# The inverse transform of a spectral layer by pairs of tiles, with two of its products as 64x64 products

## The chip, the core and the metric

The kernel runs on one core of one Trainium2 chip. The metric is the device time of one execution in microseconds (us); lower is better. The engines are named as in the profile: PE (TensorE matmul), PEld (its weight load), DVE (VectorE), ACT (ScalarE), POOL (GpSimd), SP (SyncE, which issues the DMAs).

## The reference

`x` is 2048 x 576 (S x D), in float32. The layer computes

```
def _A_ref(x, w_r, w_i):                      # spectral mixing
    X = rfft2(x)                              # over S and D: 2048 x 289 complex
    X = X * (w_r + 1j * w_i)
    return irfft2(X, s=(S, D))
def _B_ref(x, w1, w2):                        # MLP, Dff = 4608
    return maximum(x @ w1, 0) @ w2
h  = x + _A_ref(layernorm(x), w_r, w_i)
h2 = h + _B_ref(layernorm(h), w1, w2)         # the output
```

## The kernel before

The 2048 rows are held as 16 tiles (t = 0 to 15) of 128 partitions; a partition is 64 * j + h, with j = 0 or 1 the half of the tile. The FFTs are products with small matrices of cosines and sines (float32). All of the program stands in one order written by hand: each engine works through its own queue in the order of the source, and an instruction that waits holds up all that is behind it on its engine.

The program has five stages:

- the forward row transform, to 46 us;
- the middle stage (`mid_d`, `mid_b`, `mid_i`, lines 332 to 375), which transforms along D and the rest of S, multiplies by W and goes back along S; its products write column halves of 64. `mid_i` writes its result to `U` with one ACT copy for each of 16 steps (L375);
- the inverse stage (115.8 to 222.5 us, loop L641 to L673), which the change rewrites;
- plain MLP steps to 286 us;
- MLP slots with Winograd-like products (`slot`, L577) to 1046 us, and the last stores.

In the inverse stage each tile goes through these steps:

- `inv_d(t)` (L400): two PSUM halves (r = 0, 1), each the sum of a product with the 64 leftover frequencies (`lpv`, 290 columns; for r = 0 only rows 0 to 63 of it are not zero, for r = 1 only rows 64 to 127) and two with the 128 main frequencies (`dev`, 145 columns each). ACT copies the first half of each (helper L151), DVE makes difference and sum (L415, L416) and half of `y` (L419), POOL the other half of `y` (L418).
- `inv_a(t)` (L422): the row stage, `cai` (128 x 128, two 64 x 64 blocks on the diagonal, zero elsewhere) times `y`, in two products of 288 columns; DVE adds the result to `xs`, the reloaded x (L428).
- `stat2(t)` (L432): statistics of the layer norm, on DVE (L208, L209), and for every second tile the rsqrt and shift on POOL (L211 to L214).
- `norm2` (L436): the normalised tile, by ACT (L222).
- `project(t)` (L442): five transposes on PE (L446, L447); ACT copies the high part (5 x 128 columns) and a full copy (4 x 128), POOL makes the low part (L454), DVE a rest of 64 rows (L455).
- `mm1(i, a)` (L460) and `mm2(i, tt)` (L485): layer 1 and layer 2 of the MLP for weight group g and chunk c of four tiles. A product is made of three (high x high, high x low, low x high): the first product of layer 1 reads a high part that ACT wrote, the second a low part that POOL wrote.

The loop runs over t = 0 to 21: `inv_d(t)`, the start of `norm2` for a pair, `stat2(t - 3)`, `inv_a(t - 1)`, from t = 10 to 21 one unit of the MLP (two calls of `mm1` to a chunk, in two tile-iterations, then `mm2`), `project(t - 6)`, and the weight splits at t = 2, 4, 18 and 19. So layer 1 of a chunk starts a tile-iteration after the projection of the chunk's last tile. Matmuls and element-wise steps of one form have one line each in helpers: L148 is every matmul but transposes, L151 every plain ACT copy.

Buffers: PSUM has four tiles "d" of two banks, taken in turn (`ps()`), so a tile is free once its last reader four takes ago is done. "e" is a ring of ten SBUF buffers. `U` has the tag "X", which the second weight group's buffer takes over at t = 15.

Of the kernel before, what the change touches and what calls it, by code (L numbers as in the profile page):

```python
# [16 lines left out]
S, D, DFF = 2048, 576, 4608  # L17
NK = D // 2 + 1
NT = 16
# [4 lines left out]
CH = 4  # L24
# [103 lines left out]
def kernel(ctx: ExitStack, tc: tile.TileContext, x, w_r, w_i, w1, w2, cc2, c1, fb, ib, c3, out):  # L128
    nc = tc.nc
# [7 lines left out]
    n = [0]  # L137

    def ps():
        n[0] += 1  # L140
        return psum.tile([128, 1024], F32, tag="d", name=f"d_{n[0]}", bufs=4)

    def ebuf(shape, dt=F32):
        e = sb([128, EW], "e", EB, dt)[:, :int(np.prod(shape[1:]))]
        return e.rearrange("p (a b) -> p a b", a=shape[1]) if len(shape) == 3 else e

    def mm(o, l, r, start, stop):
        nc.tensor.matmul(o, l, r, start=start, stop=stop)  # L148

    def act(o, i, **kw):  # L150
        nc.scalar.activation(o, i, AF.Copy, **kw)  # L151
# [16 lines left out]
    caf, cai = ccs[:, :384], ccs[:, 384:]  # L168
# [194 lines left out]
    def mid_i(p):  # L363
        Y = Ys.pop(p)
        pu = ps()
        for e in range(2):
            ibe = IB[p // 4][:, p % 4, e, :]
            for h in range(2):
                for g in range(2):
                    mm(pu[64 * g:64 * g + 64, 512 * e + 128 * h:512 * e + 128 * h + 128],  # L370
                       dims(Y, NK * e + 128 * g + h, [2, 64]), ibe, True, True)
            for g in range(2):
                mm(pu[64 * g:64 * g + 64, 512 * e + 256:512 * e + 320],
                   dims(Y, NK * e + 225, [1, 64]), ibe[:, 64 * g:64 * g + 64], True, True)
        act(dims(U, 2 * p, [32, 2], [64, 160], [1, 2]), dims(pu, 0, [512, 2], [2, 160], [1, 2]))  # L375

    for i in range(NP + 2):
        if i < NP:
# [19 lines left out]
    Es = {}  # L398

    def inv_d(t):  # L400
        pd = ps()
        ut = [dims(U, 64 * (32 * b + 2 * t), [1, 128]) for b in range(5)]
# [5 lines left out]
        ez = ebuf([128, 578 + D])  # L408
# [6 lines left out]
        nc.vector.tensor_sub(dims(ez, 288, R2, [-1, 144]), ea[:, :, :144], pb_[:, :, :144])  # L415
        nc.vector.tensor_add(ea, ea, pb_)  # L416
        y = ez[:, 578:]
        nc.gpsimd.tensor_sub(dims(ez, 578 + 575, [-1, 287]), e0[:, 1:288], e1[:, 1:288])  # L418
        nc.vector.tensor_add(y[:, 0:289], e0, e1)  # L419
        Es[t] = y  # L420

    def inv_a(t):  # L422
        y = Es.pop(t)
        pa = ps().rearrange("p (h n) -> p h n", h=2)[:, :, :288]
        for h in range(2):
            mm(pa[:, h], cai, y[:, 288 * h:288 * h + 288], True, True)
        xt = xs[:, t, :].rearrange("p (h n) -> p h n", h=2)
        nc.vector.tensor_add(xt, xt, pa)  # L428
# [12 lines left out]

    def project(t):  # L442
        y = Zs.pop(t)
        pz = ps()
        for b in range(4):
            nc.tensor.transpose(pz[:, 128 * b:128 * b + 128], y[:, 128 * b:128 * b + 128], ident)  # L446
        nc.tensor.transpose(pz[:, 512:640], y[:, 448:576], ident)  # L447
# [4 lines left out]
        zt = ebuf([128, 512])  # L452
        act(zt, pz[:, :512])
        nc.gpsimd.tensor_sub(dst[:, 5:9, q], zt.rearrange("p (a s) -> p a s", s=128), dst[:, 0:4, q])  # L454
        nc.vector.tensor_sub(dst[0:64, 4, q], pzv[64:128, 4], dst[64:128, 4, q])  # L455
# [4 lines left out]
    def mm1(i, a, part=None):  # L460
        g, c = steps[i]
        w1h, w1l = wts[g, 0]
        if a == 0 and not part:
            pend[i] = None if i >= WINO else ps()
        p = hid_p(i, a) if i >= WINO else pend[i][:, 512 * a:512 * a + 512]
        f = slice(128 * a, 128 * a + 128)
        ops = []
        for kt in range(4):
            ops += [(w1h, kt, kt), (w1h, kt, 5 + kt), (w1l, kt, kt)]
        ops += [(w1h, 4, 4), (w1l, 4, 4)]  # L470
        for n_, (w, kt, xk) in enumerate(ops):
            if part is None or n_ // 7 == part:
                mm(p, w[:, kt, f], xc[c][:, xk, :], n_ == 0, n_ == len(ops) - 1)
        if i >= WINO:
            return
        if a == GF - 1:
            p = pend.pop(i).rearrange("p (a s) -> p a s", a=GF)
            hh, hl = sb([128, GF, 512], "D", 4, F32R), sb([128, GF, 512], "D", 4, F32R)
            nc.scalar.activation(hh, p, AF.Relu)
            nc.vector.scalar_tensor_tensor(hl, p, 0.0, hh, op0=ALU.max, op1=ALU.subtract)  # L480
            hid[i] = (hh, hl)
# [88 lines left out]

    def store(c, hs, hd):
        if steps[-1][0] == NG - 1:
            for j in range(2):
                t, d = CH * c + 2 * hs, slice(288 * hd, 288 * hd + 288)
                nc.sync.dma_start(ov[j, :, t:t + 2, d], xs[64 * j:64 * j + 64, t:t + 2, d])

    def slot(i):  # L577
        g, c = steps[i]
# [61 lines left out]
    gen = None  # L640
    for t in range(NT + 6):  # L641
        if t < NT:
            inv_d(t)
        if t % 2 == 1 and 5 <= t <= NT + 3:
            gen = norm2(t - 5, 2)
            next(gen)
        if 0 <= t - 3 < NT:
            stat2(t - 3)
        if 0 <= t - 1 < NT:
            inv_a(t - 1)  # L650
        if t == 15:
# [3 lines left out]
        if t == 17:  # L655
            project(t - 6)
        if 10 <= t < 22:
            i, u = divmod(t - 10, 4)
            if u < 2:
                mm1(i, u)  # L660
            else:
                if i == 2:
                    mm1(3, u - 2)
                mm2(i, 2 * u - 4)
                mm2(i, 2 * u - 3)
        if 6 <= t and t != 17:
            project(t - 6)
        if t in (2, 4):
            split_weights(0, t // 2 - 1)
        if t in (18, 19):  # L670
            split_weights(1, t - 18)
        if gen:
            next(gen, None)  # L673
# [49 lines left out]
```

## Time and profile before

| | |
|---|---|
| median of three runs | 1055.14 us (1054.94 to 1055.36) |
| profiled execution | 1053.18 us |
| its span | 1051.1 us |
| PE busy | 1033.6 us, 98% |
| DVE, ACT, POOL busy | 71%, 37%, 31% |
| chain that ended last, PE's share | 94% |

The span runs from the first to the last instruction of the profiled execution; its own time is 2.1 us longer. In rows of a timeline the first number is the start in us, the second the length; products that follow each other on PE overlap a little, so the distance of two starts is what a product takes of PE's time. A bracket names the idle time before the row and what ended it.

### The profile page before, as it was taken

To read this page: it belongs to the slowest core of one execution; us is meant where nothing else is said; L and a number is where in the kernel's file an instruction comes from. 1 tells how busy PE (TensorE), PEld (TensorE's weight loads), DVE (VectorE), ACT (ScalarE), POOL (GpSimd) and SP (SyncE) were. 2 spreads that over 40 slices of the span, in tenths; PEclk is the share of its full clock that TensorE was granted. 3 is DMA by queue.
4 is the path that set the end of the run, shared out by engine and by line. 5 is a ranking of instruction groups with operands and counts; after the bars stand their busy time and mean duration, and the time that the engine had idled before them with its cause. 6 is when DMAs were issued, how large, how long until landed. Compare 5 with 4: busy or idle time off the path is not lost.

```text
span 1051.1 us, 17190 instructions
## 1 busy us (share of the span) xinstructions
PE 1033.6 (98%) x6560; PEld 924.6 (88%) x6560; DVE 751.3 (71%) x1411; ACT 389.9 (37%) x846; POOL 325.7 (31%) x436
## 2 busy tenths in 40 slices
PE   8999999999999999999999999999999999999997
PEld 7878778799999999999999999999999999999996
DVE  7587686544377777778777777778777777777775
ACT  4533243521134333333333333334343333434332
POOL 4300164311132324333333423333333323243321
PEclk9999999999999999999999999999999999999999
DMA  8931700011000110000000011000000001000025
GB/s 241 249 89 49 181 2 26 23 48 49 1 26 23 28 47 23 26 23 26 23 26 23 26 30 42 26 23 26 24 26 23 26 24 46 29 23 2 1 63 118
DMA packets 31073, 48.05 MB, mean 46 GB/s; under 512 B 2960, under 2 KB 22672, under 8 KB 30992
## 3 DMA queue, kind: packets, MB, share of 16 engines
q1 hardware_dynamic: 30992, 46.96, 16.3%
q8 instruction: 52, 0.85, 0.3%
q14 instruction: 29, 0.24, 0.1%
HBM read 42.23 MB, written 4.72 MB: 45 GB/s over the span
## 4 chain that ended last, share of the span: by engine, by line
PE 94%; DVE 2%; DMA 2%; ACT 1%; POOL 0%; issue 0%; SPq 0%; ACTq 0%; DVEq 0%; POOLq 0%
PE d L148 59%; PE d L562 34%; DMA A<-in_A_x_dram 2%; PE d L446 1%; DVE st L208 0%; DVE A L428 0%; ACT e L222 0%; DMA X<-in_A_x_dram 0%; SPq L159 0%; DVE e L307 0%; POOL r L212 0%; DVE e L252 0%; PE d L447 0%; DVE e L253 0%; DVE e L416 0%
## 5 line engine op out<-in xcount | busy, mean ns | idle before, releaser
L569 DVE TENSOR_TENSOR A<-A,d 128x576 f32<-128x576 f32 x448 | 334.5, 747 | 50.5 <-PE d L562 50.2
L562 PE MATMUL d<-X,D 128*128 128x288 f32 x2304 | 346.2, 294 | 1.4 <-DVE A L569 0.9
L562 PEld LDWEIGHTS d<-X,D 128*128 128x128 f32 x2304 | 329.0, 188 | 17.2 <-DVE A L569 1.1
L148 PE MATMUL d<-B,e 128*128 128x512 f32 x952 | 238.3, 391 | 0.4 <-DVE A L428 0.4
L148 PEld LDWEIGHTS d<-B,e 128*128 128x128 f32 x952 | 172.0, 188 | 28.7 <-ACT e L151 0.8
L537 DVE SCALAR_TENSOR_TENSOR D<-d,D 128x256 fp32r<-128x256 f32 x192 | 81.5, 424 | 122.0 <-ACT D L536 122.0
L536 ACT ACTIVATE D<-d 128x256 fp32r<-128x256 f32 x192 | 73.4, 382 | 239.6 <-PE d L148 239.6
L551 POOL TENSOR_TENSOR e<-e 128x256 f32<-128x256 f32 x64 | 47.3, 739 | 355.3 <-ACT e L550 355.3
L148 PE MATMUL d<-C,e 128*128 128x512 f32 x476 | 119.1, 390 | 0.0
L148 PE MATMUL d<-X,e 128*128 128x512 f32 x476 | 118.8, 390 | 0.0
L151 ACT ACTIVATE X<-e 128x288 fp32r<-128x288 f32 (+2 forms) x177 | 70.2, 434 | 105.6 <-PE d L562 105.6
L307 DVE TENSOR_TENSOR D<-e,D 128x512 fp32r<-128x512 f32 (+1 forms) x128 | 92.7, 724 | 19.9 <-ACT D L151 19.9
L547 POOL TENSOR_TENSOR e<-e 128x256 f32<-128x256 f32 x64 | 47.6, 744 | 173.6 <-ACT e L546 173.6
L148 PEld LDWEIGHTS d<-X,e 128*128 128x128 f32 x476 | 85.9, 188 | 13.7
L148 PEld LDWEIGHTS d<-C,e 128*128 128x128 f32 x476 | 85.8, 188 | 13.7
L151 ACT ACTIVATE D<-e 128x512 fp32r<-128x512 f32 (+1 forms) x128 | 66.7, 521 | 75.5 <-POOL e L552 71.9
L307 DVE TENSOR_TENSOR X<-e,X 128x288 fp32r<-128x288 f32 (+2 forms) x177 | 83.1, 492 | 0.9 <-ACT X L151 0.9
L562 PEld LDWEIGHTS d<-X 128*128 128x128 f32 x384 | 58.0, 188 | 5.1
L562 PE MATMUL d<-X 128*128 128x288 f32 x384 | 61.4, 295 | 0.0
L148 PE MATMUL d<-e,D 128*128 128x288 f32 x384 | 53.8, 297 | 0.3 <-DVE D L480 0.3
L148 PEld LDWEIGHTS d<-e,D 128*128 128x128 f32 x384 | 52.2, 188 | 1.4 <-DVE D L480 0.6
L552 POOL TENSOR_TENSOR e<-e,e 128x256 f32<-128x256 f32 x64 | 50.4, 788 | 5.0
(79 smaller groups left out, 986.9 us busy)
## 6 DMA issues: line engine op xcount, KB each, us to landing
e<-in_B_w_dram SPq DMA_DIRECT2D x18, 576.0 KB, 3.8
e<-in_B_w_dram SPq DMA_DIRECT2D x18, 512.0 KB, 3.6
A<-in_A_x_dram SPq DMA_DIRECT2D x16, 288.0 KB, 8.4
out_dram<-A SPq DMA_DIRECT2D x32, 144.0 KB, 2.5
X<-in_A_x_dram SPq DMA_DIRECT2D x12, 288.0 KB, 7.1
e<-in_B_w_dram SPq DMA_DIRECT2D x36, 64.0 KB, 3.4
B<-in_A_w_r_dram SPq DMA_DIRECT2D x15, 144.5 KB, 8.1
B<-in_A_w_i_dram SPq DMA_DIRECT2D x15, 144.5 KB, 7.0
```

The lines of the kernel that those rows point to most:

```text
L148: nc.tensor.matmul(o, l, r, start=start, stop=stop)
L151: nc.scalar.activation(o, i, AF.Copy, **kw)
L307: nc.vector.tensor_sub(l, v, h)
L446: nc.tensor.transpose(pz[:, 128 * b:128 * b + 128], y[:, 128 * b:128 * b + 128], ident)
L536: nc.scalar.activation(h, p, AF.Relu)
L537: nc.vector.scalar_tensor_tensor(l, p, 0.0, h, op0=ALU.max, op1=ALU.subtract)
L547: nc.gpsimd.tensor_sub(fs["S3"], fs["p0"][:, 0], fs["p0"][:, 1])
L551: nc.gpsimd.tensor_add(fs["S1"], fs["p0"][:, 1], fs["p1"][:, 1])
L552: nc.gpsimd.tensor_sub(fs["S2"], fs["S1"], fs["p0"][:, 0])
L562: nc.tensor.matmul(P[:, tt], l[:, q], r, start=first and n_ == 0, stop=n_ == 2, skip_group_check=not first)
L569: nc.vector.tensor_add(xt, xt, P)
```

## The change

The inverse stage goes by pairs of tiles, and two kinds of products become 64 x 64.

- **Leftover frequencies** (`left` in the new `inv_h`): the two products of a tile with `lpv` that multiplied zero rows too become four of 64 x 64: row half r of `U`'s leftover block, column half m. Each has 290 columns.
- **Row stage** (`row`): `cai`'s two blocks are used one by one, for both tiles of the pair, as four 64 x 64 products of 288 columns: row half j, column half j for an even tile, and exchanged for an odd one. `row(0)` and `row(1)` each issue four that lie in the four quarters. The rows of odd tiles hold their halves exchanged from there to the store.
- **Where things lie**: `U` is laid out by tile (640 columns each), so `mid_i` writes it with four ACT copies of 160 columns in place of one of 640 (L375, new L377). `y` is written back into the tile's block of `U`. Two tiles share a buffer "e" for the inverse, and two for the projection.
- **x reload**: 16 DMAs as before, each for 64 partitions and two tiles, now tiles t and t + 2.
- **Store**: each DMA for two tiles becomes two for one tile each, 64 in place of 32.
- **Order**: the loop runs over u = 0 to 9, with `inv_h(u)` (leftover product of the new even tile, first half of the row stage of the old pair, leftover product of the new odd tile, second half of the row stage, residual adds), `norm2` of pair u - 2, `inv_d` of both new tiles, `stat2` of both tiles of pair u - 1, weight splits at u = 1, 2 and 8, `project` of both tiles of pair u - 2, and for u = 3 to 8 two units of the MLP.

The core of the diff:

```diff
-        act(dims(U, 2 * p, [32, 2], [64, 160], [1, 2]), dims(pu, 0, [512, 2], [2, 160], [1, 2]))
+        for e in range(2):
+            for j in range(2):
+                act(dims(U, 64 * j + 32 * e + 2 * p, [128, 5], [640, 16], [1, 2]),
+                    dims(pu, 512 * e + 2 * j, [64, 5], [4, 16], [1, 2]))
...
-    for k in range(8):
-        load_x(xs, 2 * k, 2)
+    def rows(t, j):
+        k = 64 * (j ^ t % 2)
+        return slice(k, k + 64)
+    for t in range(0, NT, 4):
+        for o in range(2):
+            for j in range(2):
+                nc.sync.dma_start(xs[rows(o, j), t + o:t + o + 3:2, :], xv[j, :, t + o:t + o + 3:2, :])
...
+    def inv_h(u):
+        new = [2 * u, 2 * u + 1] if 2 * u < NT else []
+        old = [2 * u - 2, 2 * u - 1] if u else []
+        pa = {}
+        def left(t):
+            pds[t] = ps()
+            for r in range(2):
+                for m in range(2):
+                    mm(pds[t][64 * m:64 * m + 64, 512 * r:512 * r + 290],
+                       U[64 * r:64 * r + 64, 640 * t + 512 + 64 * m:640 * t + 576 + 64 * m], lpv[64 * r:64 * r + 64, r], True, False)
+        def row(k):
+            for j in range(2):
+                for t in old:
+                    h = j ^ k
+                    mm(pa[t][rows(t, j), 512 * h:512 * h + 288], cai[64 * j:64 * j + 64, 64 * j:64 * j + 64],
+                       inv_y(t)[64 * j:64 * j + 64, 288 * h:288 * h + 288], True, True)
+        for t in new[:1]:
+            left(t)
+        for t in old:
+            pa[t] = ps()
+        row(0)
+        for t in new[1:]:
+            left(t)
+        row(1)
+        for t in old:
+            xt = xs[:, t, :].rearrange("p (h n) -> p h n", h=2)
+            nc.vector.tensor_add(xt, xt, pa[t].rearrange("p (h n) -> p h n", h=2)[:, :, :288])
...
-            mm(o, ut[4], lpv[:, r], True, False)
...
-        y = ez[:, 578:]
-        nc.gpsimd.tensor_sub(dims(ez, 578 + 575, [-1, 287]), e0[:, 1:288], e1[:, 1:288])
+        y = inv_y(t)
+        nc.gpsimd.tensor_sub(dims(y, 575, [-1, 287]), e0[:, 1:288], e1[:, 1:288])
...
-                nc.sync.dma_start(ov[j, :, t:t + 2, d], xs[64 * j:64 * j + 64, t:t + 2, d])
+                for o in range(2):
+                    nc.sync.dma_start(ov[j, :, t + o, d], xs[rows(o, j), t + o, d])
...
+    for u in range(NT // 2 + 2):
+        inv_h(u) if u <= NT // 2 else None
+        if 2 <= u:
+            for _ in norm2(2 * u - 4, 2):
+                pass
+        if 2 * u < NT:
+            inv_d(2 * u)
+            inv_d(2 * u + 1)
+        if 1 <= u <= NT // 2:
+            stat2(2 * u - 2)
+            stat2(2 * u - 1)
+        if u in (1, 2):
+            split_weights(0, u - 1)
...
+        if u == 8:
+            split_weights(1, 0)
+            split_weights(1, 1)
+        if u >= 2:
+            project(2 * u - 4)
+            project(2 * u - 3)
+        if 3 <= u < 9:
+            unit(2 * u - 6)
+            unit(2 * u - 5)
```

How the order of instructions changes is seen at two places. First POOL's queue around the projection of a chunk's last tiles, before: L454 makes a low part of layer 1's input, L418 half of `y` of an inverse tile, L211 to L214 the rsqrt and shift of a pair.

```order
L454 TENSOR_TENSOR B_1285<-e_1658,B_1285 128x4x128
L418 TENSOR_TENSOR e_1670<-e_1670 128x287
L211 TENSOR_SCALAR r_1625<-mv_1624 128x2
L212 TENSOR_TENSOR r_1625<-r_1625,half_141 128x2
L214 TENSOR_SCALAR r_1625<-mv_1624,r_1625 128x1 x2
L454 TENSOR_TENSOR B_1285<-e_1722,B_1285 128x4x128
L418 TENSOR_TENSOR e_1734<-e_1734 128x287
L454 TENSOR_TENSOR B_1285<-e_1786,B_1285 128x4x128
L418 TENSOR_TENSOR e_1798<-e_1798 128x287
```

The same place after the change (L464 is the half of `y`, L493 the low part):

```order
L464 TENSOR_TENSOR X_551<-e_1778 128x287 x2
L211 TENSOR_SCALAR r_1795<-mv_1794 128x2
L212 TENSOR_TENSOR r_1795<-r_1795,half_141 128x2
L214 TENSOR_SCALAR r_1795<-mv_1794,r_1795 128x1 x2
L493 TENSOR_TENSOR B_1333<-e_1813,B_1333 128x4x128 x2
L464 TENSOR_TENSOR X_551<-e_1889 128x287 x2
```

Before, low parts and halves of `y` alternate tile by tile, and every fourth step the rsqrt stands between them; after, both halves of `y` of a pair come first, then the rsqrt of the pair ahead of it, then both low parts of the pair that is projected.

Second, PE's queue ahead of a layer 1, with the engines that each instruction waits for, before: L446 and L447 are a tile's transposes, the products with X an inverse tile, those with cc the row stage, those with B the start of layer 1.

```order
L446 MATMUL d_1779<-ident_62,e_1622 128x128 [waits DVE_49,Activation_49]
L446 MATMUL d_1779<-ident_62,e_1622 128x128 x3
L447 MATMUL d_1779<-ident_62,e_1622 128x128
L148 MATMUL d_1791<-e_549,X_551 128x290 [waits DVE_49]
L148 MATMUL d_1791<-e_549,X_551 128x145 x2
L148 MATMUL d_1791<-e_549,X_551 128x290
L148 MATMUL d_1791<-e_549,X_551 128x145 x2
L148 MATMUL d_1811<-e_1734,cc_73 128x288 [waits DVE_49]
L148 MATMUL d_1811<-e_1734,cc_73 128x288 [waits Pool_49]
L148 MATMUL d_1815<-B_1285,e_1334 128x512 [waits DVE_49,Activation_49]
L148 MATMUL d_1815<-B_1285,e_1334 128x512 [waits Pool_49]
L148 MATMUL d_1815<-B_1285,e_1335 128x512
```

And after (the main products of two inverse tiles, L483 and L484 for the transposes of two tiles, then layer 1):

```order
L148 MATMUL d_1749<-e_549,X_551 128x145 x4
L148 MATMUL d_1760<-e_549,X_551 128x145 x4
L483 MATMUL d_1806<-ident_62,e_1771 128x128 [waits DVE_49,Activation_49]
L483 MATMUL d_1806<-ident_62,e_1771 128x128 x3
L484 MATMUL d_1806<-ident_62,e_1771 128x128
L483 MATMUL d_1817<-ident_62,e_1771 128x128 [waits DVE_49,Activation_49]
L483 MATMUL d_1817<-ident_62,e_1771 128x128 x3
L484 MATMUL d_1817<-ident_62,e_1771 128x128
L148 MATMUL d_1827<-B_1333,e_1418 128x512 [waits DVE_49,Activation_49]
L148 MATMUL d_1827<-B_1333,e_1418 128x512 [waits Pool_49]
L148 MATMUL d_1827<-B_1333,e_1419 128x512
```

Before, an inverse tile and the row stage of another stand between the last transposes and layer 1; after, layer 1 follows directly on the transposes of the chunk's last two tiles.

More of the change, by code (lines that the diff above doesn't have):

```diff
@@ L397, with inv_y @@
     xc = [xc01[:, 0], xc01[:, 1], xc2]
-    Es = {}
+    pds, Ez = {}, {}
+    def inv_y(t):
+        return U[:, 640 * t:640 * t + D]
+    def inv_h(u):
[25 more added lines that the diff above has]
+            nc.vector.tensor_add(xt, xt, pa[t].rearrange("p (h n) -> p h n", h=2)[:, :, :288])
     def inv_d(t):
-        pd = ps()
-        ut = [dims(U, 64 * (32 * b + 2 * t), [1, 128]) for b in range(5)]
+        pd = pds.pop(t)
+        ut = [dims(U, 640 * t + 128 * b, [1, 128]) for b in range(4)]
         for r in range(2):
             o = pd[:, 512 * r:512 * r + 290]
-            mm(o, ut[4], lpv[:, r], True, False)
             for h in range(2):
                 mm(o[:, 145 * h:145 * h + 145], ut[2 * ((r + h) % 2) + r], dev[:, 2 * r + h], False, h == 1)
-        ez = ebuf([128, 578 + D])
+        if t % 2 == 0:
+            Ez[t // 2] = ebuf([128, 4 * 289])
+        ez = Ez[t // 2][:, 578 * (t % 2):578 * (t % 2) + 578]
         pdv = pd.rearrange("p (r n) -> p r n", r=2)
@@ L416, in inv_d @@
         nc.vector.tensor_add(ea, ea, pb_)
-        y = ez[:, 578:]
-        nc.gpsimd.tensor_sub(dims(ez, 578 + 575, [-1, 287]), e0[:, 1:288], e1[:, 1:288])
+        y = inv_y(t)
+        nc.gpsimd.tensor_sub(dims(y, 575, [-1, 287]), e0[:, 1:288], e1[:, 1:288])
         nc.vector.tensor_add(y[:, 0:289], e0, e1)
[L420 to L428, printed above, removed]
     Zs = {}
@@ L451, in project @@
         act(dst[:, 0:5, q], pzv[:, :5])
-        zt = ebuf([128, 512])
+        if t % 2 == 0:
+            Ez[t] = ebuf([128, 1024])
+        zt = Ez[t - t % 2][:, 512 * (t % 2):512 * (t % 2) + 512]
         act(zt, pz[:, :512])
@@ L572, in store @@
         if steps[-1][0] == NG - 1:
+            t, d = CH * c + 2 * hs, slice(288 * hd, 288 * hd + 288)
             for j in range(2):
-                t, d = CH * c + 2 * hs, slice(288 * hd, 288 * hd + 288)
-                nc.sync.dma_start(ov[j, :, t:t + 2, d], xs[64 * j:64 * j + 64, t:t + 2, d])
+                for o in range(2):
+                    nc.sync.dma_start(ov[j, :, t + o, d], xs[rows(o, j), t + o, d])
     def slot(i):
@@ L638, with unit @@
     steps = first + [(g, c) for g in range(2, NG) for c in range(NC)]
[L640 to L651, printed above, removed]
+    def unit(k):
+        i, q = divmod(k, 4)
+        if q < 2:
+            mm1(i, q)
+        else:
+            if i == 2:
+                mm1(3, q - 2)
+            mm2(i, 2 * q - 4)
+            mm2(i, 2 * q - 3)
+    for u in range(NT // 2 + 2):
[11 more added lines that the diff above has]
+            split_weights(0, u - 1)
+        if u == 7:
             load_weights(1)
@@ L654 @@
             xc.append(tail[0][:, :4608].rearrange("p (a n) -> p a n", a=9))
[L655 to L673, printed above, removed]
+        if u == 8:
[7 more added lines that the diff above has]
+            unit(2 * u - 5)
     for i in range(3, len(steps)):
```

## The prediction

> **What bounds the kernel now.** I read the page first, then the windows of the inverse stage (115.84 to 222.48 us, first inverse product to last projection), PE's waits there, and the timelines of the engines that feed it. The page's engine list, its PE entry leading:
> ```profile
> PE 1033.6 (98%) x6560; PEld 924.6 (88%) x6560; DVE 751.3 (71%) x1411; ACT 389.9 (37%) x846; POOL 325.7 (31%) x436
> ```
> PE is the bound. Stage windows: window, length, then busy us (instructions) of PE, PEld, DVE, ACT, POOL, SP; granted clock; DMA share; GB/s:
> ```profile
> 115.84:222.48 106.64, 102.37 (x595) 88.02 (x593) 71.84 (x147) 44.67 (x70) 45.79 (x63) 1.00 0.18 50
> ```
> PE waits 4.3 of 106.64 us, DVE, ACT and POOL are 67, 42 and 43% busy. What remains of PE's waits (total us, count, longest):
> ```profile
> PE d L446 <- ACT e L222: 2.0, 1, 2.0
> PE d L148 <- DVE e L419: 1.1, 2, 0.9
> ```
> So the tile-by-tile order leaves PE nearly no hole. Fewer PE columns are a gain only if the new order keeps it so.
>
> **The change part by part.**
>
> *PE work.* PE timeline (start, length, instruction; runs merged), the middle stage's column-half products, then one inverse tile and its neighbours:
> ```profile
> 59.51 2.14 PE L148 MATMUL d<-e,A 128*64 128x290 f32 x24
> 61.48 1.14 PE L148 MATMUL d<-e,C 128*64 128x289 f32 x8
> ...
> 121.16 2.13 PE L148 MATMUL d<-e,X 128*128 128x290 f32 x12
> 123.12 1.13 PE L148 MATMUL d<-e,cc 128*128 128x288 f32 x4
> 124.10 2.13 PE L148 MATMUL d<-e,X 128*128 128x290 f32 x12
> ...
> 155.74 0.60 PE L446 MATMUL d<-ident,e 128*128 128x128 f32 x4
> 156.18 0.27 PE L447 MATMUL d<-ident,e 128*128 128x128 f32 x1
> 156.29 2.13 PE L148 MATMUL d<-e,X 128*128 128x290 f32 x12
> ```
> An inverse tile takes 1.96 us start to start for 1160 columns, 580 of them leftover (.98); its row stage .98. Either becomes four 64x64 products of as many columns, each on a quarter of the array: half as long, .49, if all four run at once; as long as now if only two do. That column halves run at once the trace shows (24 records in 1.97 us, with twice the columns of the 12 in 1.96); row halves stand nowhere in it. So PE's work falls by 16 x (.49 + .49) = 15.7 us, or by 0. I take 15.7, since the nearest row shows full overlap. Remaining PE work of the stage: 100.8 - 15.7 = 85.1, where 100.8 are the stage's products at their start-to-start times, without the overlap that the 102.37 count twice.
> The 121.16 row runs .17 us past the start at 123.12, a drain at most. The Trainium skill, page "TensorEngine Tiling (Array Packing)", section Key Properties, says that a change of the tiling mode drains TensorE, which speaks against the change. Seventeen switches into quarters at .17 would add 2.9 us, to about 1089; my sum holds nothing for it.
>
> *The new order's waits.* I followed all four queues through the stage in the order in which the two kernels issue, with start-to-start times from rows and handoffs of .2 us (from PE and ACT) or .12 (from DVE and POOL). For before this gives 107.4 us, .8 over the trace. For the new order it gives 129.1: 85.1 of PE work and 44.0 of waiting. Corrected by .8: 128.3, which is **+21.7**. The rows behind it, DVE:
> ```profile
> 127.19 0.45 DVE L415 TENSOR_TENSOR e<-e,d 128x288 f32<-128x288 f32 x1
> 127.68 0.46 DVE L416 TENSOR_TENSOR e<-e,d 128x290 f32<-128x290 f32 x1
> 128.17 0.46 DVE L419 TENSOR_TENSOR e<-e 128x289 f32<-128x289 f32 x1
> 128.55 0.81 DVE L208 BATCH_NORM_STATS2 st<-A 128x6 f32<-128x288 f32 x2
> 129.39 0.21 DVE L209 BATCH_NORM_AGGREGATE mv<-st 128x2 f32<-128x12 f32 x1
> 129.52 0.74 DVE L428 TENSOR_TENSOR A<-A,d 128x576 f32<-128x576 f32 x1
> 130.18 0.45 DVE L415 TENSOR_TENSOR e<-e,d 128x288 f32<-128x288 f32 x1
> ```
> POOL, then ACT:
> ```profile
> 139.86 0.23 POOL L211 TENSOR_SCALAR r<-mv 128x2 f32<-128x2 f32 x1 [0.51 <-DVE mv L209]
> 140.17 0.71 POOL L212 TENSOR_TENSOR r<-r,half 128x2 f32<-128x2 f32 x1
> 140.99 0.50 POOL L214 TENSOR_SCALAR r<-mv,r 128x1 f32<-128x1 f32 x2
> 141.45 1.27 POOL L454 TENSOR_TENSOR B<-e,B 128x512 fp32r<-128x512 f32 x1
> 142.67 0.91 POOL L418 TENSOR_TENSOR e<-e 128x287 f32<-128x287 f32 x1
> ```
> ```profile
> 137.76 0.70 ACT L151 ACTIVATE B<-d 128x640 fp32r<-128x640 f32 x1 [1.96 <-PE d L447]
> 138.36 0.59 ACT L151 ACTIVATE e<-d 128x512 f32<-128x512 f32 x1
> 138.84 0.86 ACT L222 ACTIVATE e<-A,r 128x576 f32<-128x576 f32 x1
> 139.77 0.41 ACT L151 ACTIVATE e<-d 128x290 f32<-128x290 f32 x1
> ```
> *Layer 1.* Now it follows in the iteration that projects its last two tiles (u = 3, 5, 7; before, one tile-iteration later), and needs their low parts from POOL (L454, new L493). On POOL these stand behind the rsqrt work (L211 to L214) of the next pair, which waits for DVE's statistics, and these stand on DVE behind two inverse tiles. From the end of the row stage's second half: first inverse tile on PE .98, handoff .2, ACT .36 (its .41 row to the next start), handoff .2, so DVE starts at 1.74 (its residual adds, 2 x .66, are done by then); two tiles at 1.36 end at 4.46; statistics 2 x .97 at 6.40; handoff .12 and POOL's rsqrt 1.59 at 8.11; two low parts at 1.25 at 10.6; PE goes on at 10.7. PE is done with its inverse products at 1.96 and with two projections of .55 at 3.06, waits till 4.58 for ACT's four copies (.6 and .5 in turn, the third of them the last it needs), issues one product, .23, and waits from 4.81 to 10.74: 1.5 + 5.9 = 7.45. Three times: **22.3**. Behind the waiting product PE's whole queue stands still; DVE and ACT run dry behind it.
> *First iterations.* The row stage of a pair follows directly on its inverse products. At u = 1 and 2 it waits for POOL's half of the second tile: that tile's DVE work ends its second step at 3.10 + .98, POOL's .88 and two handoffs make 5.2, PE is there at 2.45: 2 x 2.75. At u = 2 the transposes wait .8 for the norms; at u = 3 the leftover product .9 and the row stage 4.8, since its PSUM tile is released by the projection's DVE step (L455, new L494), queued behind two statistics and a weight split. Sum **12.0**.
> *After layer 1, and u = 8.* A leftover product needs the PSUM tile that the relu split still reads. Groups by form (count | busy, mean ns | idle before):
> ```profile
> L479 ACT ACTIVATE D<-d 128x1024 fp32r<-128x1024 f32 x8 | 8.2, 1026 | 45.9 <-PE d L148 45.8
> L480 DVE SCALAR_TENSOR_TENSOR D<-d,D 128x1024 fp32r<-128x1024 f32 x8 | 9.8, 1225 | 28.8 <-ACT D L479 28.8
> ```
> Some .2 + 1.0 + .2 + 1.2 us, against .98 of other work: 1.64 twice, and .57 twice ahead of layer 2. At u = 8 weight group 1 is split behind two statistics right ahead of its first use (3.8) and the norms come late (1.4). Together 9.6. In all 22.3 + 12.0 + 9.6 = 44.
>
> *Middle stage.* One ACT copy of 640 columns (.70 as in the 137.76 row) becomes four of 160, each at most the .41 of the 290-column row: up to .95 more per step. ACT idles between these copies, and PE reads them only after the last step, where warm-up products stand; without that cover the last two steps would show, 1.9. I take +.2 (bounds 0 and 1.9). The reload of x keeps its 16 transfers and bytes, in pieces half as long, and its first reader, the first residual add, comes later than now: 0; if a late piece showed, it would be inside the first iterations' waits.
>
> *Stores.* SP's queue, a weight load's two transfers and the last six stores:
> ```profile
> 94.83 1.16 SPq L301 DMA_DIRECT2D e<-in_B_w_dram  x2
> 1044.40 3.94 SPq L575 DMA_DIRECT2D out_dram<-A  x6
> ```
> Six issues take 3.94 us (.66 each). The same bytes are now twelve issues of half the size; a 64-partition issue above takes .58. Twelve at .63, between the two, take 7.6, so **+3.6** behind the last add; the ends are 0, if an issue of half the size takes half, and +3.9 at .66 each.
>
> *Clock.* The new waits hold PE idle for 4.8 and three times 5.9 us at a stretch, longer than any in the stage now. The longest in the forward stage, 2.14 us, was harmless (PE timeline); a cold start shows in the first 2 us, with 10 matrix records against 21 four us later (windows):
> ```profile
> 20.64 1.53 PE L148 MATMUL d<-cc,e 128*128 128x256 f32 x6 [2.14 <-DVE e L254]
> ```
> ```profile
> 1.35:3.35 2.00, 2.00 (x10) 2.00 (x11) 0.00 (x0) 0.85 (x2) 0.00 (x0) 1.00 0.47 141
> 5.35:7.35 2.00, 2.00 (x21) 2.00 (x20) 1.03 (x3) 0.68 (x1) 1.62 (x5) 1.00 0.85 261
> ```
> About half rate for some 3.8 us loses 1.9 us each. I take three such events, **+5.7**, bounds 0 and 4 x 1.9 = 7.6.
> The Trainium skill, page "TensorE: Matmul & The Clock Gate", Part 1, has the clock halved after a wholly idle window of about 3.4 us until a busy window has passed; by it all four gaps would count, and the sum would be 1.9 higher, near 1088.
>
> **Sum.** 21.7 + .2 + 3.6 + 5.7 = 31.2. The profiled execution took 1053.18 us (span 1051.1 and 2.1 around it): 1084.4. The median of the runs shown, 1055.14, lies 1.96 above it: 1086.3, so 1086.
>
> **The rivals.**
> *The clock holds* (the idle stretches do not slow PE): 1086.3 - 5.7 = 1080.6. For it: the granted clock reads 1.00 in every slice, even at the cold start. Against it: the record counts above.
> *Quarters run only two at once.* The 15.7 us are not saved, but the same queues followed with .98 in place of .49 hold 5.9 less waiting, since PE arrives later: 1086.3 + 15.7 - 5.9 = 1096. For it: no row half in the trace; against it: column halves overlap fully.
> *Not slower: POOL's string is short.* The page counts spans on POOL as rough. If rsqrt and low parts free their readers early, and DVE's statistics run ahead, layer 1's string of 10.7 shrinks. It decides where the low parts are there by PE's 4.8: then PE waits 0 to 1.5 per layer 1 instead of 7.45, and with the early waits halved to 6 and the 9.6 as they are, the stage idles 15.6 to 20.1 instead of 44, its clock kept. That is 1080.6 less 28.4 to 23.9, or 1052 to 1057. Against it: 4.46 of the string are DVE and ACT rows alone, and the order puts the low parts behind the statistics whatever POOL takes.
> The change does what it says on PE, whatever comes of it; that the waits do not exist is this last rival.
>
> **How the numbers follow.** Forecast 1086, chance .55; clock holds .20; two at once .13; not slower .06; the rest, unforeseen, .06. The low end: the forecast without the clock's 5.7, with half of the early waits (6.0) and half of the stores' term (1.8): 1072.8, taken as 1072. The high end: two at once, 1096, with the clock's fourth event: 1098. Differences under 0.2%, some 2.1 us, cannot be told from none. Faster than that .05 and within it .02, from the last rival and the rest; slower .93.
>
> **What would show it.** Right: PE waiting three times some 6 us at layer 1's second product for POOL's L493, with L211 to L214 of a later pair straight ahead of it; an inverse stage some 20 us longer though PE's busy time there falls; leftover and row-stage products in half the time; twelve stores behind the last add. Wrong: PE's waits in the stage under 20 us, or quarter products as long as now, or record counts unchanged behind the long waits.

## The result and the profile after

The changed kernel takes 1091.6 us (median of five runs, 1090.64 to 1092.23) against 1055.14 us: a ratio of 1.0348, 95% interval 1.0334 to 1.0362, or 36.5 us slower. The forecast was 1086 (1072 to 1098). The profiled execution took 1092.21 us with a span of 1090.1: 39.0 over the profiled execution before, against 31.2 in the sum. Two executions of the runs below lie far outside the rest and stay out of the ratios: one of the kernel before, beside e1 to e4 (2681.59 us), and one of e3's four (1169.45; the median of its other three is 1079.97).

The page's engine list for the kernel after:

```profile
PE 1037.6 (95%) x6688; PEld 918.6 (84%) x6688; DVE 749.4 (69%) x1411; ACT 391.9 (36%) x894; POOL 328.7 (30%) x436
```

The inverse stage, from its first product to the MLP product behind its last projection, in the window view:

```profile
116.05:257.82 141.77, 106.17 (x721) 82.00 (x721) 69.69 (x146) 43.41 (x69) 47.60 (x62) 0.88 0.16 39
```

The stage is 35.1 us longer; PE idles 35.6 of it in place of 4.3, and its granted clock is .88 in place of 1.00. DVE and POOL have as much work as before (69.7 and 47.6 us against 71.8 and 45.8): the time is lost in waiting and in the clock, not in work. PE's waits, the six largest groups (total us, count, longest):

```profile
PE d L148 <- POOL B L493: 11.2, 2, 5.6
PE d L148 <- POOL C L493: 5.6, 1, 5.6
PE d L148 <- DVE B L494: 3.6, 2, 3.2
PE d L148 <- ACT B L151: 2.7, 2, 1.3
PE d L148 <- DVE X L307: 2.6, 1, 2.6
PE d L148 <- DVE D L519: 2.5, 2, 1.2
```

The first two are layer 1 waiting three times for POOL's low parts. PE's timeline at the first of them, from the first record of layer 1 to the next pair:

```profile
149.38 0.49 PE L148 MATMUL d<-B,e 128*128 128x512 f32 x1 [1.33 <-ACT B L151]
155.42 8.02 PE L148 MATMUL d<-B,e 128*128 128x512 f32 x27 [5.55 <-POOL B L493]
163.37 0.72 PE L148 MATMUL d<-e,X 64*64 64x290 f32 x8
163.91 0.67 PE L148 MATMUL d<-X,cc 64*64 64x288 f32 x8
```

One record of layer 1 is issued after 1.33 us of waiting, the next after 5.55 more. POOL's timeline at that place names what stood ahead of the low parts:

```profile
148.95 0.91 POOL L464 TENSOR_TENSOR X<-e 128x287 f32<-128x287 f32 x1 [0.45 <-DVE e L462]
151.29 0.23 POOL L211 TENSOR_SCALAR r<-mv 128x2 f32<-128x2 f32 x1 [1.44 <-DVE mv L209]
151.61 0.72 POOL L212 TENSOR_TENSOR r<-r,half 128x2 f32<-128x2 f32 x1
152.43 0.50 POOL L214 TENSOR_SCALAR r<-mv,r 128x1 f32<-128x1 f32 x2
152.88 2.48 POOL L493 TENSOR_TENSOR B<-e,B 128x512 fp32r<-128x512 f32 x2
```

POOL itself idles 1.44 us for DVE's statistics, does the rsqrt of another pair, and only then makes the low parts that PE is waiting for.

The clock is read in windows behind the long waits (the last three numbers of a row are the granted clock, the DMA share and GB/s):

```profile
136.90:149.00 12.10, 7.30 (x53) 5.11 (x50) 8.31 (x20) 5.61 (x11) 6.98 (x10) 0.86 0.00 0
155.40:160.00 4.60, 4.58 (x13) 3.69 (x14) 0.00 (x0) 0.00 (x0) 0.00 (x0) 0.63 0.01 4
190.10:195.00 4.90, 4.84 (x11) 3.80 (x12) 0.00 (x0) 0.00 (x0) 0.01 (x1) 0.50 0.00 0
195.00:202.00 7.00, 5.76 (x37) 3.96 (x39) 1.23 (x1) 2.49 (x3) 0.00 (x0) 0.90 0.00 0
226.00:232.00 6.00, 5.81 (x17) 4.65 (x18) 0.00 (x0) 0.00 (x0) 0.14 (x1) 0.62 0.00 0
241.70:257.80 16.10, 16.10 (x84) 14.42 (x85) 5.85 (x8) 2.78 (x4) 4.65 (x6) 0.82 0.25 78
```

In each, PE works at less than full rate for part of the time; the first row begins ahead of its wait of 3.2 us, and its clock falls at 141.7, when PE is at work again. What a row loses is its length times what is missing of the clock: 1.7 + 1.7 + 2.5 + .7 + 2.3 + 2.9 = 11.8 us.

Last, the stores at the end, on SP's queue:

```profile
1079.52 8.26 SPq L615 DMA_DIRECT2D out_dram<-A  x13
```

Thirteen issues take 8.26 us, .64 each. From the stage's end to the span's end it is 832.3 us (1090.1 - 257.82) against 828.6 before (1051.1 - 222.48): +3.7.

### The profile page after: what moved, and what is told of

Same layout as the page of the kernel before. It is cut to its first block, busy times and chain, and to the rows that moved or that the text cites. A ratio compares the mean times of both kernels' runs of the same rounds, so it can differ in the third digit from the quotient of the medians.

```text
span 1090.1 us, 17543 instructions
## 1 busy us (share of the span) xinstructions
PE 1037.6 (95%) x6688; PEld 918.6 (84%) x6688; DVE 749.4 (69%) x1411; ACT 391.9 (36%) x894; POOL 328.7 (30%) x436
## 4 chain that ended last, share of the span: by engine, by line
PE 91%; DVE 5%; POOL 2%; ACT 1%; issue 1%; DMA 0%; SPq 0%; DVEq 0%; ACTq 0%; POOLq 0%
PE d L148 58%; PE d L601 32%; DVE st L208 1%; DVE e L462 1%; DVE X L465 1%; DVE e L461 0%; POOL B L493 0%; POOL r L212 0%; ACT e L222 0%; DVE D L519 0%; ACT D L518 0%; DVE mv L209 0%; DMA X<-in_A_x_dram 0%; DVE A L443 0%; PE d L483 0%
## 5 line engine op out<-in xcount | busy, mean ns | idle before, releaser
L148 PE MATMUL d<-B,e 128*128 128x512 f32 x952 | 242.4, 396 | 13.8 <-POOL B L493 11.2
L148 PEld LDWEIGHTS d<-B,e 128*128 128x128 f32 x952 | 175.2, 192 | 43.8 <-POOL B L493 11.8
L519 DVE SCALAR_TENSOR_TENSOR D<-d,D 128x1024 fp32r<-128x1024 f32 x8 | 9.8, 1224 | 65.3 <-ACT D L518 65.3
```

## The experiments

The theory: the new order puts layer 1 right behind the low parts that POOL makes last, and the long waits cost clock on top; the quarters save work. The rivals: the quarters themselves cost (two at once, or by changes of shape); POOL's own work is the bound in whatever order; the clock is not lost. The runs stand on several chips, on which the kernel before had medians of 1053.5 to 1055.4; so the ratios to it on the same chip are compared.

**e1, leftover quarters alone in the old order.**

```diff
-            mm(o, ut[4], lpv[:, r], True, False)
+            for m in range(2):
+                mm(pd[64 * m:64 * m + 64, 512 * r:512 * r + 290], ut[4][64 * r:64 * r + 64, 64 * m:64 * m + 64],
+                   lpv[64 * r:64 * r + 64, r], True, False)
...
```

Both halves' leftover products also move ahead of the main ones.

> The kernel before, tile by tile as it was, with one edit: the two leftover products of a tile become four 64x64 products. Theory A (four quarters run at once, and the loss of the change comes from its order alone): 16 x .49 = 7.8 us less PE work and no new wait, since the order is the old one; less some .05 us per tile for changing between the two shapes, so 1046 to 1050 us against 1055. Theory B (products in quarters run two at once, or every change of shape drains TensorE for .17 us or more): 0 to +5 us, 1055 to 1060.

Measured: 1053.94 us, ratio .9987 (.9978 to .9997), between the two. PE's timeline, an inverse tile and the next row stage:

```profile
121.76 1.91 PE L148 MATMUL d<-e,X 64*64 64x290 f32 x16
123.50 1.13 PE L148 MATMUL d<-e,cc 128*128 128x288 f32 x4
```

Leftover and main products together take 1.74 us here where they took 1.96; the quarters alone should have brought 1.47. So some .27 of the .49 us goes back for changing to 64x64 and back. What stands ahead takes some .09 more as well (a row stage 1.07 to the next start in place of .98, five transposes .63 in place of .55), so the price in this order is nearer .36, and a tile gains some .13: about 2 us in all. The stage of e1's profile is 1.0 shorter (105.7 us); the rest is not accounted for. The kernel after shows the same without that mixture: a batch of four groups of quarters, then the main products of two tiles.

```profile
177.27 0.72 PE L148 MATMUL d<-e,X 64*64 64x290 f32 x8
177.81 0.67 PE L148 MATMUL d<-X,cc 64*64 64x288 f32 x8
178.29 0.67 PE L148 MATMUL d<-e,X 64*64 64x290 f32 x8
178.78 0.67 PE L148 MATMUL d<-X,cc 64*64 64x288 f32 x8
179.37 2.25 PE L148 MATMUL d<-e,X 128*128 128x145 f32 x16
181.47 0.60 PE L483 MATMUL d<-ident,e 128*128 128x128 f32 x4
```

Start to start the inner groups take .48 and .49: all four quarters run at once. The first takes .54, the last .59 and the two main products 2.10 in place of 1.96: .3 us for one change there and back. The quarters run at once, as theory A has it, but the price of the change was expected at .05 and is .3.

**e2 and e10, the changed products in the order of before.** The loop of the kernel before, `left(t)` ahead of `inv_d(t)`, and the row stage of two tiles at even t; tiles in the order 0, 2, 1, 3 of a chunk.

```diff
+            left(t)
             inv_d(t)
...
-        if 0 <= t - 1 < NT:
-            inv_a(t - 1)
+        if t % 2 == 0 and 2 <= t <= NT:
+            row(t - 2)
```

> The changed kernel's products (leftover and row stage in quarters, y in U) in the order of the kernel before: one inverse tile per step, statistics, projection and MLP units at their old lags, and the row stage of two tiles in every second step. Tiles go in the order 0, 2, 1, 3 of each chunk, so that a pair is (0, 2) or (1, 3) and both tiles of a store have the same halves exchanged: 32 store DMAs and the old x reload. Theory A (the pair order makes all of the loss): 15.7 us less PE work, some 3 us given back for row stages that wait for y in the first steps and for changes of shape: 1040 to 1046. Theory B (quarters bring a cost of their own, in shape changes or in waits of two residual adds in a row): 1052 or more.

> The kernel of e2 once more with five rounds, for an interval: its profiled execution was 3.0 us under that of the kernel before, its median 5.7 us under. If the stage's own gain is the whole difference, 3 to 4 us faster than before (ratio .9962 to .9972); if something outside the stage helps too, 5 to 6 us (.9943 to .9953).

Measured: 1049.67 us, ratio .9947 (.9931 to .9963), and again 1049.04, ratio .9954 (.9941 to .9966): about 5 us faster than before. The same products that come with 36 us of loss in the pair order bring a gain in the old one; so the loss is the order's, with its stores (e6). The gain is smaller than the 9 to 15 expected. The shape changes 24 times there and back, some 7 to 9 of the 15.7 us; the stage of e10's profile is 4.8 us shorter (116.56 to 218.39), so 2 to 4 more are not accounted for.

e2 and e10 are one kernel, and their executions fall into two groups, 1048.7 to 1049.1 and 1050.2 to 1050.3. Their profiles come from one group each (1050.21 and 1049.06 us). In both PE waits 2.0 us for the same norm, and the product group behind that wait takes, in e2 and then in e10:

```profile
193.26 4.95 PE L148 MATMUL d<-e,D 128*128 128x288 f32 x24
193.61 3.43 PE L148 MATMUL d<-e,D 128*128 128x288 f32 x24
```

The granted clock is .50 from 194 to 196 us in e2 and 1.00 there in e10. So the same wait cost 1.5 us of clock in one execution and none in another.

**e3, projection ahead of the statistics.**

```diff
+        if u >= 2:
+            project(2 * u - 4)
+            project(2 * u - 3)
         if 1 <= u <= NT // 2:
             stat2(2 * u - 2)
             stat2(2 * u - 1)
...
-        if u >= 2:
-            project(2 * u - 4)
-            project(2 * u - 3)
```

> The changed kernel with one edit: in each iteration the projection of pair u-2 is issued ahead of the statistics of pair u-1, so on POOL the low parts stand ahead of the rsqrt work and on DVE the projection's step ahead of the statistics. Theory A (layer 1 waits for the statistics' string through POOL's order): the low parts end some 3 us earlier, each of the three 5.6 us waits falls to 2.5 to 3, and the clock loss behind them mostly goes, while the norms of the next pair come .7 later on DVE: 9 us of waits and 4 to 7 of clock, 1092 - 13 to 16 = 1076 to 1079. Theory B (the low parts wait for ACT and POOL's own work, whatever the order): 1089 to 1093.

Measured: 1080.65 us, ratio 1.0238 (1.0220 to 1.0256): 11 us less. POOL's timeline at the same place, and PE's waits:

```profile
148.76 2.48 POOL L493 TENSOR_TENSOR B<-e,B 128x512 fp32r<-128x512 f32 x2
151.33 0.23 POOL L211 TENSOR_SCALAR r<-mv 128x2 f32<-128x2 f32 x1
```

```profile
PE d L148 <- POOL B L493: 5.6, 2, 3.1
PE d L483 <- ACT e L222: 3.8, 3, 2.0
PE d L148 <- POOL C L493: 2.5, 1, 2.5
```

The low parts now start at 148.8 and the rsqrt comes behind them; the three waits fell from 16.8 to 8.1 us. The time is 1 to 2 us above theory A's 1076 to 1079, and the waits fell as it said. Not as expected: the clock fell behind 2.5 us waits too (.91 for the stage), and the norms cost PE 2 us more.

**e4, the MLP units one pair iteration later.**

```diff
-        if 3 <= u < 9:
-            unit(2 * u - 6)
-            unit(2 * u - 5)
+        if 4 <= u < 10:
+            unit(2 * u - 8)
+            unit(2 * u - 7)
```

> The changed kernel with one edit: the MLP units run one pair iteration later (u = 4 to 9 in place of 3 to 8), so that layer 1 follows a pair iteration after its last projection. Theory A (layer 1's waits are those for the low parts of its own iteration): the three waits of 1.3 + 5.6 us go (-20.7) and the clock loss behind them (-6 to -7); in exchange the iteration u = 3, without a unit to work on, may wait up to 6 us at the row stage: 1066 to 1072. Theory B (other waits come late behind them: DVE and POOL set the pace of an iteration): 1080 or more.

Measured: 1064.3 us, ratio 1.0086 (1.0068 to 1.0104): 27 us of the 36.5 go with three changed lines, some 2 more than theory A's range allowed. PE's waits in the stage:

```profile
PE d L148 <- DVE B L494: 5.8, 3, 3.2
PE d L483 <- ACT e L222: 3.0, 2, 1.9
PE d L148 <- DVE D L519: 2.5, 2, 1.2
PE d L148 <- DVE X L465: 2.3, 4, 0.7
```

No wait for POOL is left. What remains against before: the stage's waits come to 15.5 us in place of 4.3, two thirds of them in the first iterations; the granted clock is .50 behind two of them (141.5 to 146.3 and 153.2 to 156.5 us, some 4 us of work); and the stores cost 3.7.

**e5, the long waits filled.** Transposes that nobody reads, behind the last product ahead of the wait:

```diff
                 mm(p, w[:, kt, f], xc[c][:, xk, :], n_ == 0, n_ == len(ops) - 1)
+            if a == 0 and i < 4 and n_ == int(i == 3):
+                for _ in range((44, 44, 44, 18)[i]):
+                    nc.tensor.transpose(pend[i][:, 512:640], ident, ident)
```

> The changed kernel with its long waits at layer 1 filled: behind the product ahead of the wait stand 44 transposes of the identity (chunks 0 to 2, some 4.8 us at .11 us each, shorter than the wait of 5.6) and 18 at the fourth layer 1, written to a PSUM half that is not in use; nothing else changes and no result is touched. Theory A (a wait also costs half of the clock for some 3 to 6 us behind it, some 10 us in all): the waits for POOL remain as long, the products behind them run at full rate, and the time falls by 8 to 10 us: 1082 to 1084. Theory B (what follows the waits is slow for another reason, such as products whose inputs come one by one): no change, or the transposes come on top: 1091 to 1094.

Measured: 1083.62 us, ratio 1.0279 (1.0264 to 1.0294); the span is 1081.2 against 1090.1. PE's timeline at the first layer 1:

```profile
149.66 0.50 PE L148 MATMUL d<-B,e 128*128 128x512 f32 x1 [1.33 <-ACT B L151]
150.00 4.96 PE L515 MATMUL d<-ident 128*128 128x128 f32 x44
155.71 6.42 PE L148 MATMUL d<-B,e 128*128 128x512 f32 x27 [0.74 <-POOL B L493]
```

The products behind the wait start as late as before (155.7 against 155.4) but take 6.42 us in place of 8.02. The granted clock of e5's profile falls in this stage only at 141.6 us, in the wait of 3.2 us that was left unfilled. More work made the kernel shorter, by 8.9 us in the spans, 8.0 in the medians and 7.3 by the ratios: theory A.

**e6, the stores joined again.**

```diff
-                for o in range(2):
-                    nc.sync.dma_start(ov[j, :, t + o, d], xs[rows(o, j), t + o, d])
+                nc.sync.dma_start(ov[j, :, t:t + 2, d], xs[64 * j:64 * j + 64, t:t + 2, d])
```

> The changed kernel with the stores of the kernel before: one DMA for two tiles, 32 in place of 64 (the exchange of the halves of odd tiles is left out at the store, so their rows come out in exchanged halves). Theory A (the twelve issues behind the last add cost 3.6 us more than six): 1087.5 to 1088.5. Theory B (the issues were hidden behind the last products or the landing of the last bytes sets the end): 1090.5 to 1092.

Measured: 1088.42 us, ratio 1.0324 (1.0308 to 1.0339); the span is 1086.4, 3.7 under that of the change (3.2 by the medians, 2.5 by the ratios). Its last six stores:

```profile
1079.71 3.94 SPq L614 DMA_DIRECT2D out_dram<-A  x6
```

Theory A: an issue takes .66 us with two tiles here and .64 with one in the change.

**e7, the pair order with the old products.**

```diff
-            for r in range(2):
-                for m in range(2):
-                    mm(pds[t][64 * m:64 * m + 64, 512 * r:512 * r + 290],
-                       U[64 * r:64 * r + 64, 640 * t + 512 + 64 * m:640 * t + 576 + 64 * m], lpv[64 * r:64 * r + 64, r], True, False)
+            for r in range(2):
+                mm(pds[t][:, 512 * r:512 * r + 290], U[:, 640 * t + 512:640 * t + 640], lpv[:, r], True, False)
...
+            for t in old:
+                mm(pa[t][:, 512 * k:512 * k + 288], cai, inv_y(t)[:, 288 * k:288 * k + 288], True, True)
```

> The changed kernel's order, buffers and DMAs with the old products: the leftover frequencies as two products of 128x128 and the row stage with the whole cai for each tile (rows are not exchanged, the same 16 loads and 64 stores move them). Theory A (the loss is the order's, and the quarters do save work): 15.7 us more PE work, less 8 changes of shape there and back at .34 us, less 5.9 us of waits into which the longer work falls: +7, with the clock lost a little less: 1096 to 1100. Theory B (the quarters themselves are what cost): less than the 1091.6 of the change.

Measured: 1099.64 us, ratio 1.0433 (1.0415 to 1.0450): .85% or 9 us over the change by the ratios, 5.9 by the two spans (1096.0 against 1090.1). The old products make it worse, so the quarters are a gain here as well; the order with its buffers and stores, on the old products, costs some 45 us.

**e8 and e9, fewer changes of shape in the old order.** e8 issues the leftover products of the next two tiles right behind the row stage, e9 that of the next odd tile.

```diff
                        inv_y(t)[64 * j:64 * j + 64, 288 * h:288 * h + 288], True, True)
+        for m in (n + 3, n + 4):
+            if m < NT:
+                left(m)
```

> The tile-by-tile order with quarters (e2), with one edit: the leftover products of the next two tiles are issued right behind the row stage of a pair, so that all quarter products of two tiles stand in one batch and the shape changes 10 times there and back in place of 24. Theory A (each change there and back costs the .34 us that the records around it show: .09 ahead, .05 between the first two passes, .09 and .11 behind): 14 x .34 = 4.8 us less than e2's 1049.7: 1044 to 1046. Theory B (two leftover products held in PSUM so early leave the projections and the MLP units too few of the four tiles, and PE waits for them): 1049 or more.

> The tile-by-tile order with quarters (e2), with one edit: the leftover product of the next odd tile alone is issued right behind the row stage, that of an even tile stays ahead of its own inverse product. Theory A (PSUM was what e8 lacked, a change of shape costs .34 us there and back): 8 changes fewer than e2, -2.7 us, and one tile more of PSUM free than in e8: 2 to 3 us under e2. Theory B (one leftover product ahead is already too many for the four PSUM tiles): 1 to 4 us over e2.

Measured: e8 1057.9 us, ratio 1.0035 (1.0022 to 1.0048); e9 1050.22, ratio .9958 (.9945 to .9972). PE's waits in e8:

```profile
PE d L483 <- ACT e L222: 4.1, 3, 2.0
PE d L148 <- DVE A L437: 2.6, 2, 1.3
PE d L148 <- DVE X L460: 2.2, 2, 1.7
PE d L148 <- DVE e L457: 1.3, 4, 0.5
PE d L483 <- DVE A L437: 1.3, 1, 1.3
```

In e8 transposes and MLP products wait for the residual adds (L437), and leftover products and once layer 1 for an inverse tile's last reader (L457), to free a PSUM tile, which they did not in e2: theory B. For e9 neither theory came true: 2 to 3 us under e2's kernel had been expected, or 1 to 4 over, and it takes the same time. Its median is 1.2 us over e10's on the same chip, but the intervals overlap, and the difference is one of groups: three of its five executions lie near 1050.3 against one of e10's, and the lower groups are 1049.1 to 1049.3 and 1048.7 to 1049.1. Of the 2.4 us (8 x .3) that fewer changes of shape should save, 1.7 go into waits for norms (4.1 us in all, 2.4 in e10). In its profiled execution, one of the upper group, the clock fell behind one of them:

```profile
190.00:193.00 3.00, 0.97 (x9) 0.73 (x8) 1.95 (x5) 1.94 (x3) 1.02 (x1) 1.00 0.00 0
193.00:197.00 4.00, 4.00 (x22) 4.00 (x21) 1.33 (x4) 1.95 (x3) 1.53 (x2) 0.58 0.02 4
```

**e11 and e12, the norm of one pair earlier, in e2's order and in the kernel before.** Both have one wait of 2.0 us, for a norm that stands on ACT behind a projection's copies.

```diff
+        if t == 16:
+            next(gen, None)
         if 6 <= t and t != 17:
             project(t - 6)
```

> The tile-by-tile order with quarters (e2), with one edit: at t = 16 the second norm of the pair (positions 10 and 11) is issued to ACT ahead of the projection of position 10 in place of behind it. In e2 PE waits 2.0 us for that norm, and in some executions (e9's profile) the granted clock falls to .50 for 3.4 us behind it. Theory A (the norm waits only for its place in ACT's queue, and the wait costs 2.0 us and at times 1.7 of clock): 1046.5 to 1047.5 in all executions, 2 to 3.5 us under e2's 1049.0 to 1050.3. Theory B (the norm is late because POOL's rsqrt is): as e2, 1049 to 1050.

> The kernel before, with the edit of e11 alone (the second norm of the pair 10, 11 ahead of the projection of tile 10). Theory A: the wait of 2.0 us goes, and with it the upper of the two times near which the kernel before falls (1053.4 and 1055.3, 1.9 apart): 1051 to 1052 in all executions, ratio to before about .997 to .998. Theory B: 1053 to 1055 as before, the two times have another cause.

Measured: e11 1046.94 us (1046.51 to 1047.07), ratio .9934 (.9920 to .9947), the fastest of all; e12 1051.69 (1051.21 to 1051.84), ratio .9975 (.9966 to .9984). PE's waits in e11's stage:

```profile
PE d L148 <- DVE X L457: 1.4, 1, 1.4
PE d L148 <- DVE D L516: 0.7, 1, 0.7
PE d L480 <- ACT e L222: 0.4, 2, 0.2
```

Theory A for both. For the executions of the kernel before beside e12 the record gives the mean granted clock: .999 at 1053.3 to 1053.5 us, .996 to .998 at 1053.8 to 1055.4. With that wait out of the way, the changed products in the old order are worth 1051.69 - 1046.94 = 4.75 us.

## Why the prediction was right, and where it was off

- **Layer 1's waits: right.** Forecast 1.5 + 5.9 three times, 22.3; measured 1.33 + 5.6 three times, 20.8, with the named instructions in the named order on POOL. e3 and e4 take the order away, and the waits go as far as the string says.
- **First iterations: too high.** Forecast 12.0. The row stage waited 1.2 and 1.1 us at u = 1 and 2 (not 2.75 each, and by the trace for DVE's half of y, not for POOL's), 1.1 for the norms at u = 2, and .6 + .6 + 3.2 at u = 3: 7.9 idle in all.
- **After layer 1, and u = 8: 7.0 idle against 9.6.** Of the difference of 8.4 between 44.0 and 35.6 a part is only counting: the 44 run from start to start, the 35.6 from the modelled end of a record, some .2 later at each of over 20 waits.
- **The signs:** the waits, the quarters and the stores came as named. But the stage is 35.1 us longer, not some 20, and PE's busy time there did not fall: it rose from 102.4 to 106.2, since 11.8 of it is the slower clock. Without that it is 94.4.
- **Quarters: right.** .49 a group, four at once; e7 bears out the sign, e1 and e2 that they gain without the new order. "Two at once" is refuted.
- **Changes of shape: left out of the sum.** The sum held nothing for them and named the Trainium skill's rule ("TensorEngine Tiling (Array Packing)", Key Properties) with 2.9 us; the trace bears the rule out with .3 us there and back, some 2.7 for the nine batches. That this is near the 2.9 is luck: that sum has seventeen changes into quarters at .17, and the order has nine. In the pair order that is little; in the old order, with 24, it takes half of what the quarters save.
- **Stores and middle stage: right.** +3.7 against +3.6 (e6: 3.7 in the span), and the middle stage is .2 longer (116.05 against 115.84 at its end).
- **Clock: the mis-sized term.** "I take three such events, +5.7": by the windows it is 11.8, of which e5 wins back 7 to 9 by filling four of five waits. The events were five, since the waits of 3.2 us at u = 3 and 2.6 at u = 8 counted too, and the dearest cost 3.2 (2.5 + .7 in two rows), not 1.9. By 6 us this term is most of the 8 by which the sum fell short. In the stage, forecast 27.4 longer and found 35.1, 6.1 are clock and 2.7 changes of shape; by difference the waits gave some 1 us back. The forecast called the 2.14 us wait of the forward stage harmless; that holds for the profile it read, and not for seven others (see the last section). The rival "the clock holds", with the granted clock's 1.00 at the cold start as its ground, is refuted.
- **The base: luck.** The median is 5.3 us above the forecast, the profiled execution 7.8. The difference is the 1.96 us between profile and median of the kernel before, which the sum added; the change's own median lies .6 under its profile.
- **"POOL's string is short"** is refuted: POOL's work took what its rows of before said. Of PE's 5.55 us some 4.1 are its rsqrt and low parts, and 1.4 its wait for DVE's statistics ahead of them.

## What to carry to other kernels

When work is grouped into larger steps, follow each in-order queue through the new order: what a waiting instruction needs may now stand behind another step's work on an engine that is itself half idle, and such a wait can cost many times what the grouping saves. Change products and order apart: here the products gained 5 us in the old order, and the new order with its stores lost some 45. Look at the granted clock behind every wait of TensorE of some 2 us and more: here those of 2.5 us and more cost 1.7 to 3.2 us beyond their length, and those near 2 us cost something in some executions and nothing in others.

## What the runs showed of the hardware

- **The clock fell after waits shorter than expected.** Waits of 5.6 us did it each time, one of 3.2, and those of 2.5 to 2.6 in the change and in e3. One of 2.0 for a norm did it in the profiles of e2 and e9, and not in those of before and of e10, which is e2's kernel. One of 1.7 did it in e8's, and in e6's the clock fell at 136.9 us behind waits of 1.1 and .6 alone. The forward stage's wait ahead of 20.7 us, 2.14 us in the kernel before and near that in all others, had a granted clock of about .50 behind it (22 to 24 us) in the profiles of e1, e5, e6, e7, e10, e11 and e12, and 1.00 in those of before, the change, e2, e3, e4, e8 and e9; the inverse stage starts .4 us later in e10 than in e2. The loss was 1.7 to 3.2 us of work for each in the change. The Trainium skill ("TensorE: Matmul & The Clock Gate", Part 1) speaks of an idle window of about 3.4 us; here waits of 1.7 to 2.6 us could be enough. What decides for a wait near 2 us is open.
- **The times of the kernel before gather near 1053.4 and 1055.3, with some between.** e12, without its 2.0 us wait, stayed within 1051.2 to 1051.8. That fits a clock that falls behind this wait in some executions: the slower executions of before have the lower mean clock, and e2 and e10 show both cases for one kernel. The profile of a slower execution of before was not taken.
- **A store's issue takes about .65 us on SP whether it carries one tile (.64) or two (.66).**
- **A change from 128x128 to 64x64 products and back costs about .3 us** (.36 in the old order), six times what e1's expectation held for it; the four quarters of a group run at once, in .49 us. The price is read from rows: no run with fewer changes came out faster (e8, e9).
